# Attention numerators in fp32 column halves instead of three fp32r passes, with the last stage reordered

## Chip, cores and metric

The kernel runs on one core of one Trainium2 chip. The metric is the device time of one execution in microseconds (us); lower is better. Given are the median of three runs and one execution with the hardware profiler on.

## The reference, cut to what matters

One token-mixing layer, `g * attention + (1 - g) * feed-forward`, on x of shape (1, 2048, 640), all in fp32, with 32 heads of 20 features.

```python
pq = einsum("bhsd,hdf->bhsf", q, w_phi)            # pk the same with k
phi_q = concatenate([softmax(pq), softmax(-pq)])   # 40 features a head
kv  = einsum("bhsf,bhsd->bhfd", phi_k, v)          # 32 blocks of 40 x 20
z   = einsum("bhsf->bhf", phi_k)
num = einsum("bhqf,bhfd->bhqd", phi_q, kv)
den = einsum("bhqf,bhf->bhq", phi_q, z)[..., None] + 1e-6
a = (num / den).transpose(0, 2, 1, 3).reshape(B, S, D) @ wo
b = einsum("bsf,fd->bsd", silu(einsum("bsd,df->bsf", x, w1)), w2)
return sigmoid((x * gate_w).sum(-1, keepdims=True)) * a + (1 - g) * b
```

## The kernel before, in words

**Precision.** Most products are made in fp32r, a reduced form of fp32, in three passes (`PASSES`, L59): a number is split into a high part (a rounded copy, on ScalarE) and a low part (number minus high part, on VectorE or GpSimd; `split`, L119 to L122), and TensorE adds high x high, high x low and low x high into one PSUM tile. A few small products and the transposes are plain fp32.

**Stages.** First the keys and values of all 16 tiles of 128 tokens, their feature maps, and kv (to about 188 us); then the feed-forward for four blocks of 512 tokens, whose gated result waits in DRAM (`fb_d`); beside the last block of it the query weights are fused with w_phi, kv is transposed into the weights `kvw` (`make_kvw`, L889), and the first four query tiles are opened. The **last stage** (L1111 to the end, from 577.5 us of the profile) finishes the attention. It works on eight pairs `u` of query tiles (256 tokens).

**One pair in the last stage.** Its two query tiles `t` go, one after the other, through a chain: projection pq (`q_mm`, L431: 30 fp32r matmuls), row extremes and differences on VectorE (`q_max`, `q_sub`, L415, L416, L422), exp on ScalarE (`q_exp`, L789), product with z on GpSimd (`q_norm`, L806) and its sum on VectorE (`q_norm_sum`, L809), five small operations on VectorE (`q_small`, L820 to L836), scaling on GpSimd (`q_mul`, L842). The sum `q_sum` (L793) runs beside it. Then:

- transposes (`t_mm`, L993): 22 fp32 transposes of 128 x 128 into six PSUM tiles `pT`; `t_hi` (L1004) copies the high part to SBUF on ScalarE, `t_lo` (L1010) makes the low part on VectorE;
- numerators (`n_mm`, L1130): the weights `kvw` hold, for each of ten groups j of three heads, 120 feature rows and 120 columns, of which 60 are zero; the two groups of an index i add into the same 120 rows of a PSUM tile `pn`, six passes for each i from 0 to 4, and three for the last two heads (`kvwr`). `n_hi` (L1144 to L1147) and `n_lo` (L1152, L1154) split the result into `oT`;
- output projection (`w_mm`, L1173): 16 fp32r matmuls for each of five blocks of 128 output columns, into PSUM tiles `pa`; `w_copy` (L1185) copies them to SBUF on ScalarE, `w_add` (L1196) adds the feed-forward part on GpSimd and issues the store; the last pair's sums are added on VectorE straight from PSUM (L1198).

The inputs x for later query tiles come in chunks of 512, 512 and 256 columns a pair, whose high part is made on ScalarE and whose low part on GpSimd (`xb_split`, L215, by L120 and L122).

**What sets the order.** `inorder` (L128) keeps TensorE, VectorE, ScalarE and GpSimd in the order in which the code is written, here `step(u)` for pairs 1 to 5 and `last_steps` for pairs 6 and 7; pair 0 is opened before. In `step(u)` the tiles a and b belong to pair u+1 and c to pair u+2. The pT, pn and pa tiles take turns in four PSUM banks (`single`, L95); the projections use two more double banks (`pair`). DMAs are issued by SyncE in a queue of its own.

Of the kernel before, what the change touches and what calls it, by code (L numbers as in the profile page):

```python
# [30 lines left out]
GW = GR * DH  # L31
NG = H // GR
# [30 lines left out]
def mix_kernel(ctx: ExitStack, tc: tile.TileContext, xT, wqT, wkc, wkr, wv, bd, bdc, cst, wo, w1, w1r, w2, out):  # L63
# [151 lines left out]
    def xb_split(p):  # L215
        u, c = XP[p]
        r = xb.pop(p)
        t = slot(f"xb_{u}_{c}")
        split(t[:, 0, : r.shape[1]], t[:, 1, : r.shape[1]], r, "pool")
# [56 lines left out]
    vs = [ta.tile([P, KG, P], F32R, name=f"v{k}")[:, :, :VW] for k in range(VB)]  # L276
# [453 lines left out]
    def wo_load(c):  # L730
        wor_raw[c] = r = raw(f"wo{c}")
        nc.sync.dma_start(r[:GW, :D], wo[c * GW : (c + 1) * GW, :])

    def wo_split(c):
        r = wor_raw.pop(c)
        split(WO[:GW, c, 0], WO[:GW, c, 1], r[:GW, :D])
# [152 lines left out]
    def make_kvw():  # L889

        parts = [w.rearrange("p j f -> p (j f)").rearrange("p (i q f) -> p i q f", q=4, f=KD) for w in kvw]
        for h in range(2):
            nc.gpsimd.memset(parts[h][:, :, 1:3].bitcast(F32), 0.0)  # L893
# [10 lines left out]
        for j0, n, pt in pts:  # L904
            n = min(n, 2 * NG - j0)
            i0, i1 = j0 // 2, (j0 + n) // 2
            split(
                *(part[:, i0:i1, ::3] for part in parts),
                pt[:GW, : n * KD].rearrange("p (i a f) -> p i a f", a=2, f=KD),
            )  # L910
        split(
            *(kvwr[:, h].rearrange("p (k f) -> p k f", f=REST) for h in range(2)),
# [4 lines left out]
    def kvw_of(h, j):  # L917
        return kvw[h][:, j, :] if j < 2 * NG else kvwr[:, h, :]

# [77 lines left out]
    def t_hi(u, i):  # L997
        pT = fTs[u, i]
        nj, w = (2, GW) if i < NG else (1, RC)
        if (u, i) < (0, 4):  # L1000
            f = slot(f"fT{u}_{i}")
        else:
            f = slot(f"fT{u}_{i}", fu, "u", 3) if i % 2 == 0 else slot(f"fT{u}_{i}", tb, "fT", 2)
        nc.scalar.copy(f[:w, 0, : nj * 256], pT[:w, : nj * 256])  # L1004
        fTs[u, i] = f, pT

    def t_lo(u, i):
        f, pT = fTs[u, i]
        nj, w = (2, GW) if i < NG else (1, RC)
        nc.vector.tensor_tensor(  # L1010
            f[:w, 1, : nj * 256], pT[:w, : nj * 256], f[:w, 0, : nj * 256].bitcast(F32), op=ALU.subtract
        )
        fTs[u, i] = f
# [4 lines left out]
    with inorder(PE, DVE, ACT, POOL):  # L1018
# [34 lines left out]
        kvw = [wslot(f"kvw{h}", F32R)[:GW, : 2 * NG * GW].rearrange("p (j f) -> p j f", f=GW) for h in range(2)]  # L1053
        kvwr = fu.tile([RC, 2, GW], F32R, name="kvwr")
# [40 lines left out]
        for i in range(4):  # L1095
            t_mm(0, i, bank)
            t_hi(0, i)
            t_lo(0, i)
# [17 lines left out]
    for k in range(3):  # L1116
        nc.sync.dma_start(wor[k * REST : (k + 1) * REST, :D], wo[NG * GW :, :])

    def n_mm(u, gp, a):
        if (gp, a) == (0, 0):  # L1120
            oTs[u] = tb.tile([GW, 2, NG + 1, 256], F32R, tag="oT", name=f"oT{u}", bufs=2)
# [3 lines left out]
        nj, w = (2, GW) if i < NG else (1, RC)  # L1125
        f = fTs.pop((u, i))
        n = 0
        for jj in range(nj):
            for hk, hp in PASSES:
                nc.tensor.matmul(  # L1130
                    pns[u, gp][:GW, a, :],
                    kvw_of(hk, 2 * i + jj)[:w],
                    f[:w, hp, jj * 256 : (jj + 1) * 256],
                    start=(n == 0),
                    stop=(n == 3 * nj - 1),
                )
                n += 1
# [3 lines left out]
    def n_hi(u, gp):  # L1141
        o, pn = oTs[u], pns[u, gp]
        if gp < 2:
            nc.scalar.copy(o[:, 0, 2 * gp : 2 * gp + 2, :], pn[:GW])  # L1144
        else:
            nc.scalar.copy(o[:, 0, 4, :], pn[:GW, 0])
            nc.scalar.activation(o[:, 1, 5, :], pn[:GW, 1], AF.Copy, scale=stk[:GW, 0:1])  # L1147

    def n_lo(u, gp):
        o, pn = oTs[u], pns.pop((u, gp))  # L1150
        k = slice(2 * gp, 2 * gp + 2) if gp < 2 else slice(4, 5)
        nc.vector.tensor_tensor(o[:, 1, k, :], pn[:GW, : k.stop - k.start], o[:, 0, k, :].bitcast(F32), op=ALU.subtract)  # L1152
        if gp == 2:
            nc.vector.scalar_tensor_tensor(  # L1154
                o[:, 0, 5, :], pn[:GW, 1], stk[:GW, 1:2], o[:, 1, 5, :].bitcast(F32), op0=ALU.mult, op1=ALU.add
# [4 lines left out]
    def w_mm(u, m0, n):  # L1160
# [9 lines left out]
        for a in range(n):  # L1170
            ds = slice((m0 + a) * P, (m0 + a + 1) * P)
            for k, (c, ho, hw) in enumerate(todo):
                nc.tensor.matmul(  # L1173
                    pa[:, a, :],
                    WO[:GW, c, hw, ds] if c < NG else WOR[:, ds],
                    o[:, ho, c, :],
# [11 lines left out]
    def w_out(u, m0):  # L1188
        if u < NP - 1:
            w_copy(u, m0)  # L1190
        w_add(u, m0)

    def w_add(u, m0):
        y, pa, n, cols = ws.pop((u, m0))
        if u < NP - 1:
            nc.gpsimd.tensor_tensor(y[:, :n], pa, y[:, :n], op=ALU.add)  # L1196
        else:
            nc.vector.tensor_tensor(y[:, :n], pa[:, :n], y[:, :n], op=ALU.add)  # L1198
# [11 lines left out]
    def x_next(k):  # L1210
        for p in range(xb_done[0], min(xb_done[0] + k, len(XP))):
            xb_split(p)
# [11 lines left out]
    def n_last(u):  # L1224
        n_mm(u, 2, 0)
        n_mm(u, 2, 1)
        n_hi(u, 2)

    def t_pair(u, i):
        for k in (i, i + 1):  # L1230
            t_mm(u, k)
        for k in (i, i + 1):
            t_hi(u, k)

    def n_first(u):
        n_mm(u, 0, 0)
        t_mm(u, 2)
        t_hi(u, 2)
        n_mm(u, 0, 1)
        t_mm(u, 3)  # L1240
        n_hi(u, 0)
        t_hi(u, 3)

    def n_second(u):
        n_mm(u, 1, 0)
        t_mm(u, 4)
        t_mm(u, 5)
        n_mm(u, 1, 1)

    def second_out(u):  # L1250
        t_hi(u, 4)
# [209 lines left out]
```

## Time and profile before

| what | value |
|---|---|
| median of 3 runs | 759.9 us (759.83 to 759.99) |
| the profiled execution | 760.1 us |
| its span, first to last instruction | 758.3 us |
| TensorE busy | 753.5 us, 4249 matmuls |
| VectorE, ScalarE, GpSimd busy | 371.3, 266.3, 264.4 us |
| granted TensorE clock | 0.999 of full |

The span is what the instruction trace covers; 1.8 us of the execution lie outside it. Matmuls are pipelined: the duration of one in the profile runs from its start to its modelled end, so the durations overlap, and what a matmul costs in a stream is read from how long a run of them takes in the chain that ended last.

### The profile page before, as it was taken

What the parts mean: (1) busy time and instruction counts of PE and PEld (TensorE: products, weight loads), DVE (VectorE), ACT (ScalarE), POOL (GpSimd) and SP (SyncE); (2) the same over time, 40 slices, a digit from 0 to 9 for tenths busy, and PEclk for the clock granted to TensorE, in tenths of its full rate; (3) what the DMA queues carried; (4) which work ended last, traced back from release to release, by engine and by line L of the source; (5) the groups of instructions that cost most, each with busy time, mean ns of one, the idle gap of its engine ahead of it and who ended that gap; (6) DMA issues with size and microseconds to landing.
All of it is one profiled execution on the core that took longest, in us unless ns stands there. A gap on an engine that the chain in (4) does not pass through costs nothing.

```text
span 758.3 us, 10642 instructions
## 1 busy us (share of the span) xinstructions
PE 753.5 (99%) x4249; PEld 664.2 (88%) x4249; DVE 371.3 (49%) x664; ACT 266.3 (35%) x483; POOL 264.4 (35%) x165
## 2 busy tenths in 40 slices
PE   9999999999999999999999999999999999999998
PEld 7888888888888888888888888888999999999998
DVE  4676666676641221112211122124578888787861
ACT  5444444337541311122111222124354443334341
POOL 2388777768000000000000000000356766855551
PEclk9999999999999999999999999999999999999999
DMA  7111111112650220002200014023003232111222
GB/s 255 53 54 53 53 53 53 60 47 86 206 176 1 69 84 1 1 0 72 84 0 1 1 41 155 9 81 88 2 29 131 93 104 70 55 52 43 70 70 91
DMA packets 35259, 50.17 MB, mean 66 GB/s; under 512 B 3541, under 2 KB 22885, under 8 KB 35210
## 3 DMA queue, kind: packets, MB, share of 16 engines
q1 hardware_dynamic: 35210, 49.50, 20.4%
q8 instruction: 33, 0.54, 0.3%
q14 instruction: 16, 0.13, 0.1%
HBM read 38.37 MB, written 11.11 MB: 65 GB/s over the span
## 4 chain that ended last, share of the span: by engine, by line
PE 97%; DVE 1%; DMA 1%; SPq 0%; ACT 0%; POOL 0%; issue 0%; POOLq 0%; DVEq 0%; ACTq 0%
PE acc L708 25%; PE ph L520 23%; PE kvp L472 16%; PE pq L431 9%; PE pa L1173 9%; PE pn L1130 4%; PE kv L442 2%; PE pT L993 2%; PE kvp L537 2%; PE kvp L330 1%; PE kvq L330 1%; PE pwq L233 1%; PE pwk L319 1%; DMA wvr<-wv 1%; POOL eq L842 0%; PE kvp L453 0%
## 5 line engine op out<-in xcount | busy, mean ns | idle before, releaser
L122 DVE TENSOR_TENSOR u<-ph,u 128x512 fp32r<-128x512 f32 x48 | 33.2, 692 | 187.1 <-ACT u L120 187.1
L708 PE MATMUL acc<-u,w 128*128 128x512 f32 x480 | 114.1, 391 | 0.0
L893 POOL MEMSET kvw<- 120x600 f32 x2 | 1.2, 598 | 319.8 <-PE ph L520 319.8
L708 PEld LDWEIGHTS acc<-u,w 128*128 128x128 f32 x480 | 89.7, 188 | 19.1
L520 PE MATMUL ph<-xf,w 128*128 128x512 f32 x420 | 99.8, 390 | 0.0
L523 ACT ACTIVATE ph<-ph 128x512 f32<-128x512 f32 x48 | 27.9, 582 | 191.2 <-PE ph L520 191.2
L520 PEld LDWEIGHTS ph<-xf,w 128*128 128x128 f32 x420 | 78.7, 188 | 16.7
L472 PE MATMUL kvp<-wh,xa 128*128 128x500 f32 (+1 forms) x420 | 93.1, 357 | 0.0
L472 PEld LDWEIGHTS kvp<-wh,xa 128*128 128x128 f32 x420 | 71.4, 189 | 9.9
L1173 PE MATMUL pa<-oT,wo 120*128 120x256 f32 x600 | 76.6, 280 | 0.0
L1173 PEld LDWEIGHTS pa<-oT,wo 120*128 120x128 f32 x600 | 73.5, 188 | 0.0
L708 PE MATMUL acc<-u,f 128*128 128x512 f32 x300 | 72.3, 392 | 0.0
L520 PE MATMUL ph<-xf,f 128*128 128x512 f32 x300 | 72.3, 392 | 0.0
L520 PEld LDWEIGHTS ph<-xf,f 128*128 128x128 f32 x300 | 56.4, 188 | 12.5
L708 PEld LDWEIGHTS acc<-u,f 128*128 128x128 f32 x300 | 56.2, 188 | 12.1
L806 POOL TENSOR_TENSOR ez<-eq,zbc 128x1280 f32<-128x1280 f32 x16 | 48.2, 3010 | 41.3 <-ACT eq L789 41.2
L122 POOL TENSOR_TENSOR ph<-ek,ph 128x1280 fp32r<-128x1280 f32 x16 | 47.4, 2965 | 27.0 <-ACT ph L120 27.0
L431 PE MATMUL pq<-wq,xb 128*128 128x320 f32 x360 | 55.3, 310 | 0.0
L431 PEld LDWEIGHTS pq<-wq,xb 128*128 128x128 f32 x360 | 52.9, 188 | 0.0
L472 PE MATMUL kvp<-wl,xa 128*128 128x500 f32 (+1 forms) x210 | 47.4, 356 | 0.0
L842 POOL TENSOR_TENSOR eq<-eq,sm 128x1280 f32<-128x1280 f32 x16 | 37.9, 2370 | 15.0 <-DVE sm L836 13.8
L500 POOL TENSOR_TENSOR ek<-ek,st 128x1280 f32<-128x1280 f32 x16 | 38.0, 2372 | 9.1 <-ACT v L290 6.1
(161 smaller groups left out, 1120.0 us busy)
## 6 DMA issues: line engine op xcount, KB each, us to landing
wr<-w SPq DMA_DIRECT2D x26, 320.0 KB, 3.9
xrf<-xT SPq DMA_DIRECT2D x20, 256.0 KB, 3.5
fb_d<-o SPq DMA_DIRECT2D x20, 256.0 KB, 2.4
y<-fb_d SPq DMA_DIRECT2D x16, 256.0 KB, 2.9
out<-y SPq DMA_DIRECT2D x16, 256.0 KB, 2.1
xra<-xT SPq DMA_DIRECT2D x14, 256.0 KB, 3.0
xrb<-xT SPq DMA_DIRECT2D x12, 256.0 KB, 2.7
wvr<-wv SPq DMA_DIRECT2D x5, 321.0 KB, 5.2
```

The source lines that it names most:

```text
L122: eng.tensor_tensor(lo, src, hi.bitcast(F32), op=ALU.subtract)
L330: nc.tensor.matmul(kv_cols(t, lo, hi), x_of(t)[c][:, hx, :], WKV[hw][:, c, lo:hi], start=(opens and hx == 0 and hw == 0), stop=(c == NC - ...
L431: nc.tensor.matmul(dst, xt[c][:, hx, :], w[:, c, hw, lo : lo + n], start=first, stop=(hx == 1 and c == NC - 1))
L472: nc.tensor.matmul(kv_cols(t, lo, hi), xt[c][:, hx, :], WKV[hw][:, c, lo:hi], start=(n == 0), stop=(n == 3 * NC - 1), skip_group_check=True,)
L500: nc.gpsimd.tensor_tensor(groups(e), groups(e), spread(st[:, 1, :]), op=ALU.mult)
L520: nc.tensor.matmul(ph, lhs, rhs, start=(n == 0), stop=(n == len(todo) - 1))
L523: nc.scalar.activation(hs, ph, AF.Silu)
L708: nc.tensor.matmul(acc[m], lhs, rhs, start=(f == order[0] and n == 0), stop=(f == order[-1] and n == len(todo) - 1))
L806: nc.gpsimd.tensor_tensor(ez, Q[t]["e"], zbc, op=ALU.mult)
L842: nc.gpsimd.tensor_tensor(groups(q["e"]), groups(q["e"]), spread(q["sm"][:, 2 * H : 4 * H]), op=ALU.mult)
L1130: nc.tensor.matmul(pns[u, gp][:GW, a, :], kvw_of(hk, 2 * i + jj)[:w], f[:w, hp, jj * 256 : (jj + 1) * 256], start=(n == 0), stop=(n == 3 * ...
L1173: nc.tensor.matmul(pa[:, a, :], WO[:GW, c, hw, ds] if c < NG else WOR[:, ds], o[:, ho, c, :], start=(k == 0), stop=(k == len(todo) - 1),)
```

## The change

1. **Numerators.** The transposed features are copied to SBUF as they are, in fp32 (`t_out` in place of `t_hi` and `t_lo`), and `kvw` is kept in fp32, one tensor in place of a high and a low one. For each i there are two fp32 products, one per group of three heads, each with 64 columns of weights (60 and four zeros). The first writes rows 0 to 63 of `pn`, the second rows 64 to 127: two column halves of the TensorE array, tile size (128, 64) at positions (0, 0) and (0, 64). The last two heads get 64 and 56 columns. `n_all` makes all twelve products of a pair in one go. `wo` is laid out to match, with four zero rows behind each 60, so the output projection contracts 128 rows instead of 120.
2. **Order of the last stage.** New `step` and `last_steps`: the four first transposes with their copies, projection b, the two last transposes, first output projection, all numerators, projection c, the two other output projections.
3. **Low parts of x chunks** on VectorE instead of GpSimd.
4. **Sums from PSUM.** In `last_steps` the sums of pairs 5, 6 and 7 are added on VectorE straight from PSUM; pairs 0 to 4 keep copy and GpSimd add.

The three `v` tiles are also 122 columns wide instead of a 122-column view of 128.

```diff
-    def xb_split(p):
+    def xb_split(p, lo_eng="pool"):
...
-            split(
-                *(part[:, i0:i1, ::3] for part in parts),
...
+            nc.scalar.copy(kvw[:, j0 : j0 + n, :KD], pt[:GW, : n * KD].rearrange("p (j f) -> p j f", f=KD))
...
+    def t_out(u, i):
...
+        f = f.bitcast(F32)
+        nc.scalar.copy(f[:w, : nj * 256], pT[:w, : nj * 256])
         fTs[u, i] = f
...
-        for jj in range(nj):
-            for hk, hp in PASSES:
-                nc.tensor.matmul(
-                    pns[u, gp][:GW, a, :],
-                    kvw_of(hk, 2 * i + jj)[:w],
-                    f[:w, hp, jj * 256 : (jj + 1) * 256],
...
+        for side in range(2):
+            lhs = kvw_of(i, side)
+            k = side if i < NG else 0
+            nc.tensor.matmul(
+                pns[u, gp][side * CT : side * CT + lhs.shape[-1], a, :],
+                lhs,
+                f[:w, k * 256 : (k + 1) * 256],
+                start=True,
+                stop=True,
+            )
...
+        eng = nc.vector if pa.space == PSUM else nc.gpsimd
+        eng.tensor_tensor(y[:, :n], pa[:, :n], y[:, :n], op=ALU.add)
...
+            xb_split(p, "dve")
...
     def step(u):
         a, b, c = 2 * u - 2, 2 * u - 1, 2 * u
+        x_next(2)
+        t_all(u, 0, 4)
         on(b, q_mm)
         on(a, q_norm_sum)
+        t_all(u, 4, 6)
+        spikes(b)
         on(a, q_small)
         on(b, q_norm)
         on(a, q_mul)
+        w_mm(u - 1, 0, 2)
+        w_copy(u - 1, 0)
+        w_add(u - 1, 0)
         on(b, q_sum)
+        x_next(1)
+        n_all(u)
         n_lo(u, 0)
         on(b, q_norm_sum, q_small, q_mul)
+        on(c, q_mm)
         w_mm(u - 1, 2, 2)
+        spikes(c)
+        w_copy(u - 1, 2)
+        n_lo(u, 1)
+        n_lo(u, 2)
         w_mm(u - 1, 4, 1)
+        on(c, q_sum, q_norm)
         w_copy(u - 1, 4)
+        w_add(u - 1, 2)
         w_add(u - 1, 4)
```

Three places show what the new order moves. On TensorE in `step(1)`, this is a third of pair 1's numerators before, in pieces between transposes (`fT` features, the two `kvw` the high and low weights):

```order
L1130 MATMUL pn_1_4671<-fT_2_4587,kvw_3844 120x256 x2
L1130 MATMUL pn_1_4671<-fT_2_4587,kvw_3845 120x256
L1130 MATMUL pn_1_4671<-fT_2_4587,kvw_3844 120x256 x2
L1130 MATMUL pn_1_4671<-fT_2_4587,kvw_3845 120x256
L993 MATMUL pT_4_4678<-ident,eq_4185 120x128 x2
L993 MATMUL pT_4_4678<-ident,eq_4254 120x128 x2
L993 MATMUL pT_5_4683<-ident,eq_4185 80x128
L993 MATMUL pT_5_4683<-ident,eq_4254 80x128
L1130 MATMUL pn_1_4671<-fT_3_4601,kvw_3844 120x256 x2
L1130 MATMUL pn_1_4671<-fT_3_4601,kvw_3845 120x256
```

And this is all of pair 1's numerators now, between the output projection `pa` of pair 0 and the projection `pq` of tile c:

```order
L1165 MATMUL pa_0_4567<-oT_4434,wo 128x256 x15
L1165 MATMUL pa_0_4567<-oT_4434,wor_s 128x256
L1123 MATMUL pn_0_4611<-fT_0_4485,kvw 64x256 x4
L1123 MATMUL pn_1_4617<-fT_2_4498,kvw 64x256 x4
L1123 MATMUL pn_2_4623<-fT_4_4546,kvw 64x256 x2
L1123 MATMUL pn_2_4623<-fT_4_4546,kvwr 64x256
L1123 MATMUL pn_2_4623<-fT_4_4546,kvwr 56x256
L432 MATMUL pq_4638<-wq,xb_0_4470 128x320 x2
```

The 33 matmuls of three `pn` tiles became twelve in one block, each with half the columns.

On VectorE around the same place (`eq` the exponent's input, `ez` the product with z, `sm` small sums), before:

```order
L1010 TENSOR_TENSOR fT_0_4516<-pT_0_4506,fT_0_4516 120x512
L1010 TENSOR_TENSOR fT_1_4518<-pT_1_4511,fT_1_4518 120x512
L793 TENSOR_REDUCE pq_4440<-eq_4473 128x64
L809 TENSOR_REDUCE sm_4471<-ez_4526 128x64
L1010 TENSOR_TENSOR fT_2_4587<-pT_2_4582,fT_2_4587 120x512
L1152 TENSOR_TENSOR oT_4574<-pn_0_4575,oT_4574 120x512
L1010 TENSOR_TENSOR fT_3_4601<-pT_3_4595,fT_3_4601 120x512
```

Now, from the last sum of tile a in the piece before `step(1)` into that step:

```order
L794 TENSOR_REDUCE pq_4397<-eq_4430 128x64
L123 TENSOR_TENSOR xb_0_4470<-xrb_0_4382,xb_0_4470 128x512
L123 TENSOR_TENSOR xb_2_4475<-xrb_2_4384,xb_2_4475 128x512
L810 TENSOR_REDUCE sm_4428<-ez_4467 128x64
L416 TENSOR_REDUCE mmq_4538<-pq_4506 128x32
```

The low parts of the features are gone, and low parts of x stand between the sum over `eq` and the sum over `ez`.

On GpSimd in `step(1)` and the next, before (`xb` low parts of x, `y` the sums for the output):

```order
L842 TENSOR_TENSOR eq_4572<-eq_4572,sm_4570 128x1280
L1196 TENSOR_TENSOR y_2_4744<-pac_2_4783,y_2_4744 128x512
L806 TENSOR_TENSOR ez_4808<-eq_4736,zbc 128x1280
L1196 TENSOR_TENSOR y_4_4788<-pac_4_4810,y_4_4788 128x256
L122 TENSOR_TENSOR xb_2_4920<-xrb_2_4537,xb_2_4920 128x512
L122 TENSOR_TENSOR xb_4_4925<-xrb_4_4618,xb_4_4925 128x256
L122 TENSOR_TENSOR xb_0_4930<-xrb_0_4623,xb_0_4930 128x512
```

Now:

```order
L843 TENSOR_TENSOR eq_4539<-eq_4539,sm_4537 128x1280
L807 TENSOR_TENSOR ez_4737<-eq_4671,zbc 128x1280
L1183 TENSOR_TENSOR y_2_4672<-pac_2_4712,y_2_4672 128x512
L1183 TENSOR_TENSOR y_4_4717<-pac_4_4739,y_4_4717 128x256
L807 TENSOR_TENSOR ez_4837<-eq_4814,zbc 128x1280
L843 TENSOR_TENSOR eq_4671<-eq_4671,sm_4669 128x1280
```

GpSimd loses the low parts of x, and tile c's product `ez` now stands ahead of the sum `y_2`.

More of the change, by code (lines that the diff above doesn't have):

```diff
@@ L31 @@
 GW = GR * DH
+CT = P // 2
 NG = H // GR
@@ L275, in mix_kernel @@
     VB = 3
-    vs = [ta.tile([P, KG, P], F32R, name=f"v{k}")[:, :, :VW] for k in range(VB)]
+    vs = [ta.tile([P, KG, VW], F32R, name=f"v{k}") for k in range(VB)]
     for v in vs:
@@ L889, in make_kvw @@
     def make_kvw():
-        parts = [w.rearrange("p j f -> p (j f)").rearrange("p (i q f) -> p i q f", q=4, f=KD) for w in kvw]
-        for h in range(2):
-            nc.gpsimd.memset(parts[h][:, :, 1:3].bitcast(F32), 0.0)
+        nc.gpsimd.memset(kvw[:, :, KD:], 0.0)
         pts = []
@@ L1052, in mix_kernel @@
         wo_load(4)
-        kvw = [wslot(f"kvw{h}", F32R)[:GW, : 2 * NG * GW].rearrange("p (j f) -> p j f", f=GW) for h in range(2)]
-        kvwr = fu.tile([RC, 2, GW], F32R, name="kvwr")
+        kvw = wslot("kvw")[:GW, : 2 * NG * CT].rearrange("p (j f) -> p j f", f=CT)
+        kvwr = fu.tile([RC, GW], F32, name="kvwr")
         w = make_kvw()
```

262 lines of the change are left out of this document (71 added, 191 removed).

## The prediction, made before the result was known

> **What bounds the kernel now.** First the page: the span, the busy times and the shares of the chain that ended last.
>
> ```profile
> span 758.3 us, 10642 instructions
> PE 753.5 (99%) x4249; PEld 664.2 (88%) x4249; DVE 371.3 (49%) x664; ACT 266.3 (35%) x483; POOL 264.4 (35%) x165
> PE 97%; DVE 1%; DMA 1%; SPq 0%; ACT 0%; POOL 0%; issue 0%; POOLq 0%; DVEq 0%; ACTq 0%
> ```
>
> TensorE is busy throughout, and the chain runs through it. The change acts in the last stage, so next come the windows of three steady steps there (columns: length, then busy time and count of each engine) and of the end, and what made TensorE wait from 565 us on.
>
> ```profile
> 618.66:643.15 24.49, 24.49 (x198) 24.49 (x197) 20.19 (x35) 9.74 (x19) 17.17 (x10) 1.00 0.26 82
> 643.15:667.68 24.53, 24.53 (x197) 24.53 (x197) 19.55 (x33) 9.73 (x19) 17.16 (x10) 1.00 0.18 59
> 667.68:692.21 24.53, 24.53 (x197) 24.53 (x197) 19.45 (x33) 9.31 (x18) 17.36 (x10) 1.00 0.19 59
> 743.71:758.30 14.59, 11.31 (x97) 11.11 (x95) 2.63 (x5) 1.12 (x3) 1.72 (x2) 0.96 0.24 81
> PEld pT L993 <- POOL eq L842: 0.6, 2, 0.4
> PEld pn L1130 <- DVE fT L1010: 0.2, 1, 0.2
> ```
>
> A step takes 24.5 us, all of it TensorE; VectorE has 4 to 5 us to spare, GpSimd 7, ScalarE 15. All waits of the stage for other engines come to 0.8 us. Busy time alone would prove little, as durations overlap, so I check it with pieces of the chain in order of time (start, length, matmuls):
>
> ```profile
> 571.60 1.75 PE pT L993 x16
> 577.49 2.84 PE pn L1130 x24
> 585.39 1.07 PE pn L1130 x9
> 594.02 3.71 PE pa L1173 x32
> 599.81 4.41 PE pq L431 x30
> 604.22 5.65 PE pa L1173 x48
> ```
>
> A step holds two projections (2 x 4.41), five output blocks (3.71 + 5.65), 33 numerator matmuls (2.84 + 1.07 = 3.91) and 22 transposes (22 x 1.75 / 16 = 2.41): 24.50 us, the whole step. So the stage is as long as its matmuls take in a stream. Relief on other engines is worth nothing by itself; a microsecond of TensorE is worth a microsecond, eight times over.
>
> **The change part by part.** *Numerators, removed.* 3.91 us for each of eight pairs.
>
> *Numerators, added.* Twelve plain fp32 products of 256 columns a pair. The trace has plain fp32 products in the fused weights, 30 calls in the code (six groups, five chunks):
>
> ```profile
> L233 PE MATMUL pwq<-constb,wTq 120*128 120x120 f32 x50 | 6.4, 274 | 0.0
> L233 PE MATMUL pwq<-constb,wTq 40*128 40x40 f32 x10 | 1.3, 281 | 0.0
> 511.14 1.11 PE pwq L233 x10
> 512.25 3.44 PE acc L708 x15
> 519.09 0.78 PE pkvt L900 x11
> 519.87 3.62 PE acc L708 x15
> 526.90 1.23 PE pwq L233 x10
> 528.14 3.63 PE acc L708 x15
> ```
>
> They appear 60 times: one call is two instructions. So a pair gets 24 in place of 33. Their length at 256 columns is shown nowhere. Ten of 120 columns take 1.11 us, 0.111 each, and those of 40 columns hardly less per instruction (1.23 for ten), so at this size something other than the columns sets the pace, and 0.111 is the lower end. The fp32 transposes stream 128 columns in 1.75 / 16 = 0.109; 256 columns at that pace take 0.219. I take 0.219, because a transpose is the row in which fp32 columns are streamed with short weight loads. One after the other, 24 x 0.219 = 5.26 us; that is 1.35 more than before.
>
> Here the column halves decide. A call's two instructions use the same half, the next call the other one. If different halves run side by side while instructions start in order, the first starts alone, then the second of one call runs beside the first of the next, and the last ends alone: 13 slots in place of 24, 13 x 0.219 = 2.85 us. No row of this trace shows two halves at work; bounds are 13 and 24 slots. I take 13, since the halves have different weights, different inputs and different PSUM rows, and nothing in the code makes one wait for the other. The Trainium skill, TensorEngine Tiling (Array Packing), Tiling Modes, says that tiles of the array run loads and matmuls independently; no run so far shows it here. The same page says that a change of tiling mode drains the array.
>
> *Change of shape.* The rows above let me price it. The group with 40 rows (526.90) takes 0.12 more than the one with 120 rows (511.14), though it has fewer columns; the feed-forward run behind it, and the one behind the 60-row transposes, take 3.63 and 3.62 against 3.44 behind a 120-row group. So going to a smaller shape and back costs about 0.12 + 0.18 = 0.30 us. A block of numerators goes there and back once: 0.30 a pair, between 0 (if column halves differ from row halves) and 0.30. By the page's drain the sum would be the same, so trace and rule agree.
>
> Sum: 2.85 + 0.30 - 3.91 = -0.76 us a pair, **-6.1 us** for eight.
>
> *Low parts of the features* leave VectorE, and low parts of x come to it from GpSimd:
>
> ```profile
> L1010 DVE TENSOR_TENSOR fT<-pT,fT 120x512 fp32r<-120x512 f32 x40 | 26.6, 683 | 18.3 <-ACT fT L1004 18.3
> L122 POOL TENSOR_TENSOR xb<-xrb,xb 128x512 fp32r<-128x512 f32 x12 | 16.0, 1342 | 13.1 <-ACT xb L120 13.1
> L122 DVE TENSOR_TENSOR xf<-xrf,xf 128x512 fp32r<-128x512 f32 x19 | 13.9, 779 | 17.0 <-ACT xf L120 17.0
> L555 DVE TENSOR_TENSOR u<-ur,u 128x512 fp32r<-128x512 f32 x4 | 5.0, 1245 | 2.4 <-ACT u L551 2.4
> ```
>
> A step sheds 5 x 0.683 and a smaller one, and takes two of 0.779 and one of half the size: about 19.5 - 3.8 + 2.0 = 17.7 us of some 23.7. GpSimd sheds two of 1.342 and a smaller one, some 3.4. Neither is on the path: zero, as long as the new waits below stay covered. The same subtraction took 0.779 while GpSimd was idle and 1.245 while it was busy, so I count up to 0.5 more each. The Trainium skill, SBUF — State Buffer, SBUF: two separate sides, goes further and against this edit: a VectorE operation with two SBUF inputs and a GpSimd operation lock each other out for a whole instruction. The 1.245 fits that; by it a chunk could wait up to one `ez` (3.0 us), which the late-VectorE rival below takes in.
>
> *The new order.* The two chains that must fit, from these rows:
>
> ```profile
> L415 DVE TENSOR_REDUCE mmq<-pq 128x32 f32<-128x640 f32 x12 | 9.8, 816 | 0.9 <-PE pq L431 0.8
> L789 ACT ACTIVATE eq<-eq 128x1280 f32<-128x1280 f32 x16 | 20.4, 1274 | 39.1 <-DVE eq L422 39.1
> L806 POOL TENSOR_TENSOR ez<-eq,zbc 128x1280 f32<-128x1280 f32 x16 | 48.2, 3010 | 41.3 <-ACT eq L789 41.2
> L809 DVE TENSOR_REDUCE sm<-ez 128x64 f32<-128x1280 f32 x16 | 23.6, 1478 | 2.8 <-POOL ez L806 2.7
> L842 POOL TENSOR_TENSOR eq<-eq,sm 128x1280 f32<-128x1280 f32 x16 | 37.9, 2370 | 15.0 <-DVE sm L836 13.8 <-PE pn L1130 0.8
> L827 DVE RECIPROCAL sm<-sm 128x32 f32<-128x32 f32 x16 | 5.6, 353 | 0.5
> L1152 DVE TENSOR_TENSOR oT<-pn,oT 120x512 fp32r<-120x512 f32 x16 | 10.7, 676 | 0.0
> L1152 DVE TENSOR_TENSOR oT<-pn,oT 120x256 fp32r<-120x256 f32 x8 | 3.3, 417 | 4.4 <-ACT oT L1147 4.4
> L1154 DVE SCALAR_TENSOR_TENSOR oT<-pn,stk,oT 120x256 fp32r<-120x256 f32 x8 | 3.8, 475 | 0.0
> ```
>
> Tile b: from the end of its projection to the transposes of the next step, 4 x 0.81 + 1.27 + 3.01 + 1.48 + some 1.3 for the five small operations (the longest 0.35) + 2.37 = 12.7 us. TensorE meanwhile has six transposes, an output block, the numerators, projection c and the other output blocks: 0.66 + 3.71 + 3.15 + 4.41 + 5.65 = 17.6. Slack 4.9. Second chain: the next step's first two transposes reuse the PSUM banks of the last two `pn` tiles, whose low parts stand on VectorE behind tile c's extremes: 4 x 0.81 + 0.68 + 0.42 + 0.48 = 4.8 us after projection c, against 5.65. Slack 0.8 to 1.3, the tightest place. Queued behind those low parts is the sum of tile c, for which nobody waits soon. I cost the order at zero in the steps and +0.4 at the entry, where transposes 4 and 5 and pair 1's transposes meet banks that VectorE must first empty; bounds 0 and 1.
>
> *The rest.* Sums from PSUM take ScalarE's copy and GpSimd's add out of three late pairs; SyncE's queue gets the stores of pairs 5 and 6 a little earlier; the very last sum already came from PSUM, so the tail behind the last matmul stays. Fewer splits of `kvw` and wider `wo` lie under the feed-forward (ScalarE and VectorE half idle there). Zero, within 0.2 either way.
>
> Against the profiled execution: 760.1 - 6.1 + 0.4 = 754.4; the median lies 0.2 lower, so **754.2 us**.
>
> **The rivals.** *Halves one after the other (slower).* If the array takes only one instruction at a time whatever its half, a pair takes 5.26 + 0.30 = 5.56, 1.65 more than before, eight times: +13.2, 773.1. For it: no row shows the contrary, and successive matmuls here always follow each other. Against it: those all used the same columns. The break-even is (3.91 - 0.30) / 0.219 = 16.5 slots: at least 7.5 of 24 instructions must hide.
>
> *Overlap in part, or VectorE late.* At 16 slots a pair saves 0.11, and the time is 759. VectorE a microsecond past its slack in each of six steps gives 754.2 + 6 = 760. The Trainium skill, TensorE: Matmul & The Clock Gate, Part 3, gives 2.38 for three column tiles, an efficiency of 0.79; as an estimate from it, 24 x 0.219 / (2 x 0.79) + 0.30 = 3.63, and the time 758. Together 756.5 to 763.
>
> *A cheaper fp32 pass.* At 0.111 an instruction, side by side: 13 x 0.111 + 0.30 - 3.91 = -2.17 a pair, 743; one after the other -0.95, 752.6. Against it: transposes of the same type at 0.109 for half the columns.
>
> **How the numbers follow.** Side by side as priced 0.62, with a range of its own from 752 (no cost of shape) to 756.5; one after the other 0.20, about 773; in part or late 0.12; cheaper 0.06. The range from 750.5 to 773.5 leaves out the cheap end and the upper half of the slow case. A difference of 0.2%, 1.5 us, is about what a measurement of this kernel can tell from no change. Faster 0.62 + 0.05 + 0.04 = 0.71; within it 0.07; slower 0.22.
>
> **What would show it.** Right: blocks of 24 numerator instructions in 3.0 to 3.3 us, pairs of starts a few ns apart, steps of 23.7 us with TensorE busy throughout. Wrong: blocks of 5.3 to 5.6 us (halves in turn); blocks of 3.2 us but idle TensorE ahead of `pT`, released by VectorE or GpSimd (order); feed-forward or output matmuls with another pace, which I assume unchanged.

## The result and the profile after

| | before | after |
|---|---|---|
| median | 759.85 us (759.60 to 759.99, 5 runs) | 756.58 us (756.51 to 756.98, 5 runs) |
| span of the profiled execution | 758.3 us | 754.7 us |
| last stage, from its first instruction to the end of the span | 180.8 us | 175.45 us |
| start of the last stage | 577.49 us | 579.25 us |

The ratio of after to before is 0.9958, with a 95% interval from 0.9944 to 0.9973: faster by 3.3 us, where the forecast was 5.7. The last two rows of the table say where to look. The last stage became 5.36 us shorter, close to the forecast, but it starts 1.76 us later, and nothing that stands ahead of it was meant to change in time.

The page of the changed kernel:

```profile
span 754.7 us, 10442 instructions
PE 748.6 (99%) x4177; PEld 646.7 (86%) x4177; DVE 370.0 (49%) x634; ACT 264.0 (35%) x477; POOL 243.9 (32%) x143
PE 96%; DVE 2%; DMA 1%; issue 0%; ACT 0%; SPq 0%; DVEq 0%
```

TensorE has 72 matmuls less (nine for each pair) and is still busy for 99% of the span; VectorE has a little more of the chain than before. The windows of the last stage, cut at each step's first transposes (length, then busy time and count of PE, PEld, DVE, ACT, POOL, granted clock, DMA share, GB/s):

```profile
579.25:612.98 33.73, 32.37 (x249) 29.08 (x247) 29.76 (x44) 14.36 (x27) 16.38 (x10) 1.00 0.27 85
612.98:636.68 23.70, 23.70 (x188) 22.43 (x187) 22.06 (x30) 10.06 (x18) 15.47 (x8) 1.00 0.28 85
...
707.76:754.70 46.94, 43.76 (x363) 41.03 (x360) 19.42 (x35) 11.20 (x22) 11.19 (x6) 1.00 0.25 82
```

A steady step takes 23.70 us in place of 24.5, all of it TensorE. VectorE is busy for 22.06 us of the first one and 20.8 of each of the next three, not for the 17.7 that the prediction counted, and that already costs something in the window ahead of them, where TensorE is busy for 32.37 of 33.73. The pieces of the chain in order of time (start, length, what) show both:

```profile
579.25 0.66 PE pT L990 x6
584.31 2.77 PE pn L1123 x24
592.90 2.74 DVE xb L123 x2
602.69 1.88 DVE xb L123
604.62 2.61 PE pq L432 x16
612.98 1.75 PE pT L990 x16
614.73 4.40 PE pq L432 x30
619.13 0.66 PE pT L990 x6
619.78 3.82 PE pa L1165 x32
623.60 2.74 PE pn L1123 x24
626.34 4.60 PE pq L432 x30
630.95 5.73 PE pa L1165 x48
```

From 612.98 on the chain never leaves TensorE: 1.75 + 4.40 + 0.66 + 3.82 + 2.74 + 4.60 + 5.73 = 23.70. A pair's 24 numerator instructions take 2.74 us, where 33 took 3.91. The projection behind them takes 4.60 where the one behind transposes takes 4.40, and the output blocks take 9.55 where they took 3.77 + 5.65 = 9.42. In the entry, though, the chain runs through VectorE: a low part of x (`xb`) ends just ahead of the second half of a projection.

Inside a block the 24 instructions start at 0, 6, 266, 273, 482, 489, 698, 705 ns and so on to 2429 and 2435: two by two, 6 or 7 ns apart, twelve slots of 0.216 us. So the two column halves do run side by side.

### The profile page after: what moved, and what is told of

Read it like the earlier page. It is cut to its first block, busy times and chain, and to the rows that moved or that the text cites. A ratio compares the mean times of both kernels' runs of the same rounds, so it can differ in the third digit from the quotient of the medians.

```text
span 754.7 us, 10442 instructions
## 1 busy us (share of the span) xinstructions
PE 748.6 (99%) x4177; PEld 646.7 (86%) x4177; DVE 370.0 (49%) x634; ACT 264.0 (35%) x477; POOL 243.9 (32%) x143
## 4 chain that ended last, share of the span: by engine, by line
PE 96%; DVE 2%; DMA 1%; issue 0%; ACT 0%; SPq 0%; DVEq 0%
PE acc L709 25%; PE ph L521 23%; PE kvp L473 16%; PE pa L1165 10%; PE pq L432 9%; PE pn L1123 3%; PE kv L443 2%; PE pT L990 2%; PE kvp L538 2%; PE kvp L331 1%; PE kvq L331 1%; PE pwq L234 1%; PE pwk L320 1%; DVE xb L123 1%; DMA wvr<-wv 1%
## 5 line engine op out<-in xcount | busy, mean ns | idle before, releaser
L1165 PE MATMUL pa<-oT,wo 128*128 128x256 f32 x600 | 77.8, 283 | 0.0
L1165 PEld LDWEIGHTS pa<-oT,wo 128*128 128x128 f32 x600 | 74.6, 189 | 0.8 <-DVE oT L1144 0.8
L790 ACT ACTIVATE eq<-eq 128x1280 f32<-128x1280 f32 x16 | 20.4, 1275 | 67.9 <-DVE eq L423 67.9
```

Source lines behind the costliest of these rows:

```text
L790: nc.scalar.activation(Q[t]["e"], Q[t]["e"], AF.Exp)
L1165: nc.tensor.matmul(pa[:, a, :], WO[:, c, hw, ds] if c < NG else WOR[:, ds], o[:, ho, c, :] if c < NG else o[:GW, ho, c, :], start=(k == 0) ...
```

## The experiments

The first 30 us of the program, in which all kernels built on the changed one have the same code, differ between their profiles by up to 1.1 us: the last matmul of `kvq` starts at 31.67 us in E1 and at 32.74 in E2. TensorE starts beside the DMAs of the first weights, and in E9, for one, the chain runs through the DMA of `wv`. The difference stays until the last stage, whose first transposes start at 576.59 us in E1, 576.83 in E5, 577.21 in E8 and 577.36 in E9. Where two medians differ by about that or less, the comparison is made with the trace, stage by stage.

### Why the last stage starts later: E1 and E3

The rows that got longer ahead of the last stage are matmuls on the feed-forward weights `w` and `w_r`. Before:

```profile
L708 PE MATMUL acc<-u,w 128*128 128x512 f32 x480 | 114.1, 391 | 0.0
L520 PE MATMUL ph<-xf,w 128*128 128x512 f32 x420 | 99.8, 390 | 0.0
L708 PE MATMUL acc<-u,w_r 128*128 128x512 f32 x40 | 9.8, 391 | 0.0
L708 PE MATMUL acc<-u,f 128*128 128x512 f32 x300 | 72.3, 392 | 0.0
```

After:

```profile
L709 PE MATMUL acc<-u,w 128*128 128x512 f32 x480 | 115.2, 393 | 0.0
L521 PE MATMUL ph<-xf,w 128*128 128x512 f32 x420 | 100.6, 392 | 0.0
L709 PE MATMUL acc<-u,w_r 128*128 128x512 f32 x40 | 10.0, 395 | 0.0
L709 PE MATMUL acc<-u,f 128*128 128x512 f32 x300 | 72.3, 392 | 0.0
```

Those on the weights `f` didn't change. From the start of one matmul to that of the next in its group (pauses over 300 ns left out), the mean is 228.0 before and 230.2 ns after for `acc<-u,w`, 227.9 and 229.7 for `ph<-xf,w`, and 228.9 and 233.1 for the 80 on `w_r`: 480 x 2.2 + 420 x 1.8 + 80 x 4.2 ns = 2.1 us. That is more than the delay of 1.76; the first matmuls on keys and values came 0.6 us earlier after the change than before, so the delay gathers 2.3 us between 8 and 572 us, 2.2 of them in the feed-forward. What the change did to these tiles is move them. `kvwr`, one tensor instead of a high and a low one, shrank from 960 to 480 bytes a partition, and every tile that lies behind it in SBUF slid down: some of the `w` tiles, both `w_r`, and in the last stage `oT`. In the built programs tile `w1_12`, for one, begins at byte 200416 instead of 200896: 32 bytes past a multiple of 64, where before it lay on one. `f` lies ahead of `kvwr`. With the order of the matmuls in the built programs, the tiles called `w` can be told apart in the trace: of `acc<-u,w`, the matmuls on tiles that moved take 229.1 ns before and 233.3 after, those on tiles that stayed 226.9 and 227.1. Two runs test this from both sides.

E1, the changed kernel with `kvwr` padded to its old size:

```diff
-        kvwr = fu.tile([RC, GW], F32, name="kvwr")
+        kvwr = fu.tile([RC, 2 * GW], F32, name="kvwr")[:, :GW]
```

> The changed kernel, with kvwr given back its former size of 960 bytes a partition, so that every tile behind it in SBUF stands where it stood before (0 instead of 32 modulo 64 bytes); nothing else. Theory A (the address of weights and inputs sets the pace of TensorE): the feed-forward runs on weights behind kvwr go back from about 230.3 to 228.6 ns a matmul, the last stage then starts 1.8 to 2.3 us earlier, an output block falls from 5.73 to 5.65 us a three-block run, and the time is 753.0 to 754.5 us. Rival B (the 1.8 us are the larger loads of wo, the other kvw preparation, or scatter between executions; the slower output runs come from 128 instead of 120 rows): 756.6 us, no change.

E3, the kernel before with 32 bytes more:

```diff
-        kvwr = fu.tile([RC, 2, GW], F32R, name="kvwr")
+        kvwr = fu.tile([RC, 2, GW + 4], F32R, name="kvwr")[:, :, :GW]
```

> The kernel before, with 32 bytes a partition added to kvwr, so that all tiles behind it stand 32 bytes off (32 instead of 0 modulo 64), nothing else. Theory A (addresses): feed-forward runs on those weights at about 230.3 ns a matmul, last stage 1.8 to 2.3 us later, output runs 2 ns a matmul slower, 762 to 764 us. Rival B (wo, kvw or 128 rows): 759.9 us, no change.

E1 took 753.47 us (ratio to before 0.9918, 0.9903 to 0.9932), E3 762.62 (1.0038, 1.0023 to 1.0053), both as theory A had it. The rows of E1:

```profile
L709 PE MATMUL acc<-u,w 128*128 128x512 f32 x480 | 114.1, 391 | 0.0
L1165 PE MATMUL pa<-oT,wo 128*128 128x256 f32 x600 | 77.1, 281 | 0.0
```

And of E3:

```profile
L708 PE MATMUL acc<-u,w 128*128 128x512 f32 x480 | 115.2, 393 | 0.0
L1173 PE MATMUL pa<-oT,wo 120*128 120x256 f32 x600 | 77.9, 283 | 0.0
```

The padding alone gives back 3.1 us, and 32 bytes alone cost the old kernel 2.9 us with the same durations, row by row. So it is the address of the tiles, not what the change computes. In the profiles E1 ends 3.2 us earlier than the changed kernel: 2.66 of that lie ahead of the last stage (its first transposes start at 576.59 against 579.25; 2.2 are of the feed-forward, and 0.3 of the start, which varies), and 0.5 in it, where the output blocks take 9.46 us a pair in place of 9.55. The 0.04 us a pair by which 9.46 still exceeds the old 9.42 stay also with the old addresses; they come with the wider `wo` or `oT`, and weren't taken apart.

### Do the halves need each other close by: E2

E2 is the changed kernel with the twelve products in another order, all lower halves first and then all upper halves:

```diff
+        for side in range(2):
+            for gp in range(3):
+                for a in range(2):
+                    n_mm(u, gp, a, (side,))
         for gp in range(3):
-            for a in range(2):
-                n_mm(u, gp, a)
             n_hi(u, gp)
```

> The changed kernel with the same 24 numerator instructions a pair and the same result, but all twelve of the lower half issued first and then all twelve of the upper half. Theory A (halves hide each other only when they stand next to each other in the stream): 23 to 24 slots of 0.216 us, a block of 5.1 to 5.2 us in place of 2.6, eight times +2.5, so 775 to 778 us. Rival B (the array takes matmuls of the free half from further back in its queue): block and time unchanged, 756 to 757.5 us. Rival C (the halves do not matter, the gain came from the lighter VectorE): unchanged too, but then the starts in the trace are one after the other.

It took 769.59 us (1.0127, 1.0110 to 1.0144), 13.0 more than the changed kernel: between the theory and the rival. One block of it on TensorE in order of start (start, length, what; `kvwr` with 64 columns is the last lower product of a pair, with 56 the last upper one):

```profile
626.29 2.43 PE L1123 MATMUL pn<-fT,kvw 120*64 120x256 f32 x12
628.50 0.38 PE L1123 MATMUL pn<-fT,kvwr 80*64 80x256 f32 x1
628.55 0.38 PE L1123 MATMUL pn<-fT,kvw 120*64 120x256 f32 x1
628.72 0.38 PE L1123 MATMUL pn<-fT,kvwr 80*64 80x256 f32 x1
628.77 1.67 PE L1123 MATMUL pn<-fT,kvw 120*64 120x256 f32 x7
630.28 0.60 PE L1123 MATMUL pn<-fT,kvwr 80*56 80x256 f32 x2
```

The `n_mm` of a pair's twelve products now takes the side as an argument. Ten lower instructions on `kvw` come first in the code, then two on `kvwr`, then the upper ones. Twelve on `kvw` have started when the first on `kvwr` does: two upper instructions overtook it. The starts are one by one up to the ninth (at 1777 ns), then four in pairs (1777 and 1783, 1993 and 2050, 2209 and 2266, 2429 and 2481), then one by one again: 8 + 4 + 8 = 20 slots. So a free half takes work from behind, but from at most three instructions further back, and only the four lower instructions at the seam are covered. Eight slots more, 8 x 0.216 x 8 = 13.8 us, is what was measured within 1 us. That halves can't overlap at all is refuted by the block itself, and so is that their place in the queue doesn't matter. The Trainium skill, TensorE: Matmul & The Clock Gate, Step-by-step: what each phase is for, says that only weight loads are pulled ahead and matmuls stay in program order; these rows show the contrary for two halves of the columns, so here the measurement decides.

### What the numerators are worth without the new order: E6

E6 is the kernel before, its order, low parts of x on GpSimd, copies and addresses, with part 1 of the change alone. Its numerators stand in five blocks a pair, between transposes.

```diff
-        for jj in range(nj):
-            for hk, hp in PASSES:
...
+        for side in range(2):
+            lhs = kvw_of(i, side)
+            k = side if i < NG else 0
...
     def t_lo(u, i):
-        f, pT = fTs[u, i]
...
+        pass
```

> The kernel before with the fp32 column-half numerators alone: its order (a block for each chunk, five blocks a pair), its low parts of the inputs on GpSimd, its copies, its addresses. Theory (a change of the array's shape costs about 0.35 us a block, there and back): 12 slots x 0.216 = 2.59, with five blocks 5 x 0.35 = 1.75 more and the block edges not overlapped, so 4.3 to 4.6 us a pair in place of 3.91: +3 to +6 us, 763 to 766. Rival (the change of shape is free or hides, the slots alone count): 2.6 to 3.0 us a pair, 750 to 752.5, and the order of the changed kernel is needless.

It took 760.05 us (ratio 1.0005, 0.9996 to 1.0014): no difference that can be told. Both expectations missed. A step of its chain:

```profile
658.49 1.02 PE pn L1127 x8
659.50 1.02 PE pT L990 x8
660.52 4.39 PE pq L432 x30
664.92 0.58 PE pn L1127 x4
665.50 0.58 PE pT L990 x4
...
673.00 4.60 PE pq L432 x30
...
683.28 1.02 PE pn L1127 x8
```

The step takes 683.28 - 658.49 = 24.79 us, 0.25 more than the 24.53 of before. Four instructions are two slots, 0.43 us, and take 0.58; the four transposes behind them take 0.58 where four took 0.44; the projection behind numerators takes 4.60, the other one 4.39. So each block pays about 0.15 when it begins or ends and 0.14 (ahead of transposes) or 0.20 (ahead of a projection) in what follows it: 0.29 to 0.35 for a change of shape there and back. Twelve slots and five such changes are 2.59 + 4 x 0.29 + 0.35 = 4.10 us a pair, against 3.91 before. The mechanism is that of the theory; its sum was too high because I took the block's edges as not overlapped on top of 0.35 for each change. The four steady steps cost about 1 us more; the entry, where the first pair's numerators stand mostly in one block, is 0.5 shorter than before, and the stage starts 0.46 earlier, so the time ends where it was. Part 1 becomes a gain only together with the new order, which has one block a pair. What that order would be worth with the old numerators was not run.

### The entry: E4, E5, E9 and E10

In the entry of the changed kernel, a `xb` of 128 x 256 starts on VectorE while GpSimd works on `ez` (columns as above):

```profile
601.34 2.95 POOL L807 TENSOR_TENSOR ez<-eq,zbc 128x1280 f32<-128x1280 f32 x1 [6.85 <-DVE sm L837]
602.69 1.87 DVE L123 TENSOR_TENSOR xb<-xrb,xb 128x256 fp32r<-128x256 f32 x1
```

It ends at 604.56, right after `ez` at 604.29, and TensorE's `pq` at 604.62 is what waited. All five subtractions of 128 x 256 start inside an `ez` and end 0.28 us after it; beside an idle GpSimd one takes 0.41 us (in E9, at 593.75). The whole group (minimum, median and maximum in ns) and TensorE's wait for it:

```profile
L123 DVE TENSOR_TENSOR xb<-xrb,xb x15: 679/1786/2136, 592.9 to 696.0; 128x512 fp32r<-128x512 f32 x10, 128x256 fp32r<-128x256 f32 x5
...
PE pq L432: 0.8, 1
```

The median of 1.79 us is more than the 0.779 + 0.5 that the prediction allowed. Two things could be at fault, the engine (VectorE and GpSimd hold each other up) or the place (the third low part is issued only ahead of the numerators). E4 changed both, in the changed kernel; E5 is the same with E1's padding.

```diff
-            xb_split(p, "dve")
+            xb_split(p, "pool")
...
-        x_next(2)
+        x_next(3)
...
-        x_next(1)
```

> The changed kernel with the low parts of x back on GpSimd, all three chunks of a pair at the start of the step (in the step's middle they would stand behind the long products on GpSimd). Theory A (a subtraction of two SBUF tiles on VectorE waits for a GpSimd operation under way, and in the first step TensorE waits for it): no VectorE row of 1.8 us for 128x256 is left, the wait of 0.8 + 1.1 us of projection c in the first step is gone, the steps stay at 23.7 us, 754.8 to 755.8 us. Rival B (the wait in the first step is the order's, whichever engine makes the low parts): 756.3 to 757 us or more.

> The changed kernel with both repairs at once: kvwr padded to its old 960 bytes a partition, and the low parts of the input chunks back on GpSimd, issued at the start of the step. Theory (two separate costs: the addresses 3.1 us over the whole program, the lock between VectorE and GpSimd 1.4 us in the entry to the last stage): the gains add, ratio to the kernel before 0.9918 - 0.0018, near 0.990, 752.0 to 752.5 us. Rival (one of the two gains was the other's in disguise, for example the low parts only late because the matmuls were late): no better than the padded kernel, 753.2 to 753.8.

E4 took 755.17 us (0.9941, 0.9926 to 0.9956), E5 752.15 (0.9900, 0.9886 to 0.9915), both as the theories had it. The two repairs add up: from the changed kernel to before is 0.9958, with the addresses repaired 0.9918, with both 0.9900.

E9 and E10 change one thing each, on top of E1's padding: E9 leaves the low parts on VectorE and issues all three at the step's start, E10 puts them on GpSimd and leaves the places.

> The padded kernel with all three low parts of the input chunks on VectorE, but issued together at the start of the step instead of two there and one ahead of the numerators. Theory (the low parts are long because VectorE and GpSimd hold each other up, 1.87 us in place of 0.4 while GpSimd works on ez): the place in the queue doesn't help, the subtractions stay near 1.8 us in the median, and the time is 753.2 to 754.0, as the padded kernel. Rival (the third low part is only issued too late): the 1.4 us that the move to GpSimd brought come from the earlier place, so 752.0 to 752.5.

> The padded kernel with the low parts of the input chunks on GpSimd, at the places of the changed kernel (two at the start of the step, one ahead of the numerators). Theory (the engine decides): the entry is as short as with the early place, 752.0 to 752.6, if the third part, which stands on GpSimd behind the 3.0 us of ez and the 2.37 of eq, is still in time. Rival (the place decides): behind ez and eq on GpSimd it comes later than on VectorE, and a step waits 1 to 3 us for it: 754 us and more.

E9 took 753.05 us (0.9914, 0.9899 to 0.9928), E10 772.58 (1.0181, 1.0162 to 1.0201). From the stage's first transposes to the output blocks `pa` x48 of the first step, the chain of E1 takes 604.69 - 576.59 = 28.10 us, that of E9 604.52 - 577.36 = 27.16, that of E5 603.26 - 576.83 = 26.43. So with VectorE the early place is worth 0.94 us, and in the early place the engine 0.73. Neither expectation was wholly right: the early place helps, and the median of the subtractions falls to 1.28 us in E9, but GpSimd brings something more. In E9 the low parts, three in one row, still start while GpSimd is at work on `ez`:

```profile
589.64 3.03 POOL L807 TENSOR_TENSOR ez<-eq,zbc 128x1280 f32<-128x1280 f32 x1 [5.39 <-ACT eq L790]
591.00 3.17 DVE L123 TENSOR_TENSOR xb<-xrb,xb 128x512 fp32r<-128x512 f32 x3
599.86 4.67 PE L432 MATMUL pq<-wq,xb 128*128 128x320 f32 x30 [0.66 <-DVE sm L837]
```

The three stand ahead of VectorE's work on the next tile, which is late by what they lose, and TensorE waits 0.66 us for `sm`. On GpSimd in E5 the three take 3.23 us together and nobody waits for them. In E10 the place is what hurts:

```profile
628.78 2.37 POOL eq L843
631.15 0.69 POOL y L1183
...
632.32 0.73 POOL xb L123
...
633.10 4.15 PE pq L432 x16
```

The third low part stands on GpSimd behind a scaling and a sum, and TensorE waits for it in the middle of a projection, five times, 13.4 us in all. The rival had it so, with 1 to 3 us a step, but E10 is 19.1 us slower than E1. The 16 matmuls behind the first four of these waits take 3.99 to 4.15 us, where those behind the last take 2.61: some 5.9 us more. With the waits that is 19.3 us. The windows of the half projection shown above and of the last one have the reason (columns as above, the granted clock third from the end):

```profile
633.10:637.30 4.20, 4.20 (x18) 4.20 (x19) 0.01 (x1) 0.00 (x0) 2.27 (x1) 0.59 0.63 185
715.80:718.40 2.60, 2.59 (x18) 2.59 (x19) 0.00 (x0) 0.00 (x0) 2.29 (x1) 1.00 0.35 111
```

The granted clock is 0.59 of full in the first window and 1.00 in the second, so such a wait can cost more than its length. The low parts may go to GpSimd only if they go there early.

### The sums from PSUM, and the finer address: E8, E7 and E11

E8 is E1 with part 4 undone (copy on ScalarE, add on GpSimd, `w_copy` put back at its four places in `last_steps`). That concerns pairs 5 and 6 alone: the sums of pair 7 came from PSUM in the kernel before, too, and do so in E8, other than its expectation says.

> The changed kernel with kvwr padded, and with the last sums of pairs 5 and 6 (and the first parts of the last pair) copied by ScalarE and added by GpSimd as before. Theory (that part of the change is off the path, as the prediction costed it: zero within 0.2): 753.2 to 753.8, as the padded kernel alone. Rival (the copies would hold ScalarE while the last pairs need it, or the direct sums hold VectorE): 0.5 to 2 us slower or faster than the padded kernel.

It took 754.29 us (0.9931, 0.9916 to 0.9945), 0.8 above E1 and in the rival's range. But the trace puts 0.62 of that ahead of the last stage (it starts at 577.21 against 576.59), where the code is the same. From there to VectorE's last sum, E8 takes 749.20 - 577.21 = 171.99 us and E1 748.32 - 576.59 = 171.73. So part 4 is worth about 0.3 us, a little more than the theory's 0.2: in E8, the last pair's transposes wait 0.3 us for a scaling on GpSimd that stands behind the sum.

E7 is E5 with 64 bytes more of padding behind `kvwr`, which puts the moved tiles on a multiple of 128 bytes:

```diff
-        kvwr = fu.tile([RC, 2 * GW], F32, name="kvwr")[:, :GW]
+        kvwr = fu.tile([RC, 2 * GW + 16], F32, name="kvwr")[:, :GW]
```

> As the run with both repairs, but with 64 bytes more of padding, so that the tiles behind kvwr keep their place modulo 64 bytes and change it modulo 128, 256 and 512. Theory (only the place modulo 64 bytes counts): the same time as with both repairs, within 0.4 us, and 228.0 to 228.8 ns a feed-forward matmul. Rival (a coarser grid counts as well): another pace of the matmuls on those weights, 0.5 to 3 us faster or slower.

It took 752.08 us (0.9899, 0.9883 to 0.9916), the same as E5, but not because nothing changed. From start to start, `acc<-u,w` takes 226.8 ns in place of 228.0, and the output matmuls `pa<-oT,wo` 120.2 in place of 119.6. By the trace the gain is 1.0 us up to the last stage, the loss 0.6 in it, and 0.6 went in the first 30 us. So the rule "only modulo 64 bytes" is refuted. E11 is E5 with the feed-forward tiles alone moved:

```diff
     fp = opened("fp", reuse_waits="tile")
+    fp.tile([P, 16], F32, name="fpad")
```

> Both repairs, and 64 bytes of padding ahead of the feed-forward weights alone, which puts them on a multiple of 128 bytes, while oT stays where it was. Theory (the feed-forward matmuls ran at 226.8 ns in place of 228.0 in the run with 64 bytes more for everything, and the output ones at 120.2 in place of 119.6 us per thousand because oT moved too): about 0.9 us of the feed-forward gain stays and the output keeps 119.6 ns, 751.0 to 751.7 us. Rival (the two go together, or the start-up gives it back): 752.0 to 752.3, no difference from both repairs.

E11 took 751.26 us (0.9890, 0.9875 to 0.9904), as the theory had it (its "us per thousand" reads ns a matmul). By the trace, the feed-forward is 0.97 us shorter than in E5 and the last stage as long. Its rows:

```profile
L710 PE MATMUL acc<-u,w 128*128 128x512 f32 x480 | 113.6, 390 | 0.0
L1166 PE MATMUL pa<-oT,wo 128*128 128x256 f32 x600 | 77.1, 281 | 0.0
```

This is the fastest version found: the change, with the old place of the tiles but for 64 bytes, and the low parts of x on GpSimd at the start of a step. It is 8.4 us faster than before, where the change alone was 3.3.

## Why the prediction was right or wrong

Faster, as forecast, but by 2.4 us less: two of its terms were wrong in the same direction, and a third, better than forecast, hid part of it. The time, 756.58 us, lies just outside the range that the prediction gave its main case (752 to 756.5), at the near end of that for "overlap in part, or VectorE late" (756.5 to 763). Of that rival the first half is refuted, as all twelve slots hold two instructions, and the second is true in the entry alone; most of what is missing has a cause that no rival had. That the time falls within the whole range, 750.5 to 773.5, says little about the mechanism. From the spans:

| term | forecast | measured |
|---|---|---|
| start of the program, where the kernels vary | 0 | -0.6 |
| from 8 us to the last stage, the feed-forward above all | 0 | +2.3 |
| steps: numerators, change of shape, output | -0.76 a pair, -6.1 | -0.865 a pair, -6.9 |
| stalls of the entry | +0.4 (0 to 1) | about +2.0 |
| the last two pairs, beyond their steps | 0 | -0.45 |
| sum | -5.7 | -3.6 |

The first two rows make the 1.76 us by which the stage starts later. The measured step is the mean of four (98.24 us before from 610.94 to 709.18, 94.78 after from 612.98 to 707.76). The entry is what is left of its window once two such pairs are taken off. Before, the window was this:

```profile
577.49:610.94 33.45, 33.45 (x266) 33.43 (x265) 28.25 (x46) 14.74 (x28) 23.39 (x16) 1.00 0.36 111
```

33.73 against 33.45 us is +0.28, and +0.28 + 2 x 0.865 = 2.0. Likewise for the end: -2.18 + 2 x 0.865 = -0.45.

*Side by side: right, and a little cheaper.* The twelve slots of 0.216 us make 2.59 instead of 13 x 0.219 = 2.85. The size of a slot was right, taken from transposes. The count was one too high because I let a call's second instruction hold back the next call: "if different halves run side by side while instructions start in order". They don't: the other half's first instruction starts 6 ns after the block's first, past the second instruction of the first call. E2 shows how far this goes, three instructions. The rivals "one after the other" and "cheaper fp32 pass" are out.

*Change of shape: right.* 0.30 forecast; 0.35 in the changed kernel (2.74 - 2.59, and 4.60 - 4.40 behind), 0.29 to 0.35 in E6. That the drain was priced from row groups and holds for column halves was a guess, and E6 shows it five times a pair.

*Output blocks: left out.* They take 0.13 us a pair more, 0.09 of it by the address (E1). So the numerators and the change of shape alone save 0.97 us a pair, and the output takes back a part. That the step came out within 0.1 us of the forecast is partly luck: 0.26 too much for the slots stands against 0.05 too little for the change of shape and 0.13 for the output.

*The new order, at zero in the steps: right.* No window from 612.98 to 707.76 has idle time of TensorE, and the two chains that had to fit, fit.

*Low parts of x on VectorE, "neither is on the path: zero": wrong.* The step that failed is "I count up to 0.5 more each". They took 1.79 us in the median, up to 2.14, and in the entry, where the projections follow each other closely, that reached TensorE. Of the 2.2 us of stalls from the stage's start to the first step's output blocks (27.98 us, against 25.8 of matmuls at their steady lengths), 0.6 are the banks that the prediction had priced at 0.4 and that E5 still shows, and 1.6 go with the low parts (in E1, 0.94 by their place and 0.73 by their engine). The Trainium skill, SBUF — State Buffer, SBUF: two separate sides, had this: the two engines lock each other out for a whole instruction. A `xb` that starts inside an `ez` ends 0.27 us after it, and that agrees. I cited it and then costed by two rows whose means hide the wait: of the 19 `xf` of 0.779 us one, at 164.95, took 2.48 inside a GpSimd operation and the others 0.68 or 0.69, and the four `u` of 1.245 took 0.69, 2.41, 1.19 and 0.69. One by one, the instructions of the kernel before showed the price already.

*"Feed-forward or output matmuls with another pace, which I assume unchanged": wrong,* and named there as what would make the prediction wrong. The diff shows the cause plainly, a tile with half the bytes, but I read the diff for instructions and not for addresses. E1 and E3 show it from both sides. At +2.3 us it is the largest error in the table.

*Sums from PSUM: nearly right* at zero within 0.2; E8 gives 0.3 us in their favour, from two pairs and not the three that the prediction counted. The remaining 0.15 of the last pairs wasn't taken apart.

## What to carry to other kernels

Two products with at most 64 columns each can share the array, if the two halves stand next to each other in the queue and in one block, since each change of shape costs 0.3 us and a free half looks only some three instructions ahead. When a change alters a tile's size, compare the addresses of all tiles behind it and the rows of matmuls that read them, even of stages that the change doesn't touch; a pad of a few hundred bytes was worth nearly as much as the change. And before giving VectorE work with two SBUF inputs, look at what GpSimd does at that time, and price it with GpSimd's instruction, not with its own, and not with the mean of rows of which some ran beside an idle GpSimd.

## What the runs showed of the hardware that was not expected

- The pace of matmuls depends on where their operand lies. For `acc<-u,w`, of whose weights a part was moved, the mean from start to start is 226.8 ns with the moved tiles on a multiple of 128 bytes (E7, E11 226.9), 228.0 with them 64 bytes past one (before, E1, E5, E6), 230.2 with them 32 bytes past a multiple of 64 (after, E3 230.3). For the moved tiles alone it is 226.8, 229.0 and 233.3. For `w_r`, which moved as a whole, it is 227.4, 228.8 and 233.1 as weights of `ph`. For `oT`, which is streamed against the weights `wo`, the order is not the same: 120.2 at a multiple of 128 (E7 alone), 119.6 at 64 past it, 121.1 at the odd 32; `wo` itself has the same place in all these programs. Why the place counts stays open.
- A half of the array that is free takes a matmul from further back in the queue: it starts 6 to 57 ns after one of the other half, ahead of up to three that stand before it (E2).
- An fp32 matmul instruction with 256 columns takes a slot of 0.216 us whether one half is at work or both: the lone slots of E2 are 216 ns apart, as are the pairs of the changed kernel.
- A wait of TensorE can cost its clock as well. In E10 the granted clock falls to 0.5 of full for 3.4 us within 0.6 us of the end of the first wait (4.3 us) and of each of the next three (2.27 us); behind the last one, as long, it stays at 1.00. In the changed kernel, where TensorE sits idle for at most 0.8 us at a time in the last stage, it stays there throughout. All changes of the clock in E10 lie on a grid of 3.413 us, and within one interval of it the first four waits leave TensorE idle for 1.9 us or more, the last for 1.7. That a threshold lies between the two is a guess from one run.
